# Retention chunks in another order: v scaled behind the masks, the next chunk's scores ahead, loads and copies of h in other buffers

## The chip, the core and the metric

One core of a Trainium2 chip runs the whole program. TensorE (PE) multiplies matrices from SBUF into PSUM; VectorE (DVE) and ScalarE (ACT) work element by element; GpSimd (POOL) has a small part; SyncE (SP) issues nearly all DMAs. Each engine works through its own queue in order. The metric is the device time of one execution in microseconds; smaller is better.

## What is computed

Retention (attention with a decay in place of the softmax) over 4 sequences, 8 heads, 576 positions of 64 dimensions, and behind it two layers of feed-forward, each with its own weights and function:

```python
scores = scale * np.matmul(q, k.transpose(0, 1, 3, 2))
gamma = 1.0 - 2.0 ** (-5.0 - np.arange(H))
Dmat = np.where(rel >= 0, gamma[:, None, None] ** rel[None, :, :], 0.0)
x = np.matmul(scores * Dmat, v)            # then (2304, 512): token, head and dimension
h = x @ w_in;   x = (h * np.cos(h)) @ w_out            # first layer, 512 -> 2048 -> 512
h = x @ w_in2;  x = where(h >= 1, h, where(h <= -1, 0, (h + 1) ** 2 / 4)) @ w_out2
```

All values are float32. Products are made of two parts of each operand, high and low, three matmuls for one.

## The kernel before, in words

**Tokens.** The 2304 tokens are cut into five blocks (0 and 1 have 256 and 512 tokens, the others 512) and, for retention, into 20 chunks of 128 or 64 tokens of one sequence. Chunks 0 to 6 make blocks 0 and 1, chunks 7 to 10 block 2, chunks 11 to 15 block 3, chunks 16 to 19 block 4. A *slot* is one of the 16 pieces of 128 columns of w_in for one block; the 32 slots of blocks 0 and 1 take turns and are numbered 0 to 31, of which 30 and 31 are block 1's last two.

**A chunk.** `load` fetches qk, kv and pt (a table by position). `prep` scales v by a power of gamma with the table vtb: on DVE as one instruction (line 287), in block 1 on ACT, one instruction per head (line 285). `state` multiplies k and v into a running matrix, which `add_state` adds into T (line 317; line 315 copies it for a sequence's first chunk). `scores` multiplies k and q into the banks S and O (or y0 and y1 for every second chunk of the first two blocks) and adds with `full` a part of what comes from T; `masked` multiplies by the mask msk into R (line 357); `attend` multiplies v and R and the rest of T; `post` scales by pt into xs (line 379) and splits xs into xhl, the high part on ACT (line 386) and the low part on DVE (line 387). All small matmuls of retention have line 291.

**A slot.** `mm1` multiplies xhl by wi into h, a bank of PSUM (line 413). `actA` copies h to SBUF as hs for blocks 0 and 1 (line 459) and rounds it (lines 461, 462); `actB` is a sine and a square (467, 468); `actC` multiplies by h (482) and splits the result into gh on ACT (474) and gl on POOL, for a few slots on DVE (475). `mm2` multiplies gh and gl by wo (428 to 430), two slots later. `evac` copies a finished block to st and stores it as yd.

**Weights.** They come as 64-bit words. A piece of w_in or w_out is loaded as raw (line 116, from the fifth piece on with a second copy rsh, line 122); `convert` makes C from it on DVE (149, 153), X on ACT (132), W and X on DVE (139, 140), the high part on ACT (155) and the low part on DVE (156), and the result is kept as wi or wo; wi is also stored as wd (163) for later blocks. During blocks 0 and 1 the first layer's weights are made; from block 2 on the second layer's.

**Order.** Lines 687 to 717 write out the start: loads for chunks 0 to 6 and four raw pieces, then chunk after chunk, with three conversions between. Block 2's chunks and later ones are put by a plan (`at`) at steps between slots: a load, `prep` one step before `scores`, `masked`, `attend`, `post`. A scheduler then orders the instructions of each engine by what they depend on and by its own estimate of time; a note `behind(later, earlier)` fixes an order for it, without a wait on the chip. It may move an instruction far ahead if nothing holds it. Pools set how many buffers a name has: qkv and pt (pool ap) two, x (xp) five, which hold xhl and hs, st (stp) four, raw and rsh (cv) two each.

## Time and profile before

| what | value |
|---|---|
| median of 3 runs (902.56, 901.92, 905.1) | 902.56 us |
| the profiled execution: its time, its span | 903.84 us, 902.0 us |
| busy share of the span: PE, DVE, ACT, POOL | 94%, 64%, 49%, 12% |
| DMA moved, mean | 210.87 MB, 234 GB/s |
| chain that ended last, by engine | PE 84%, DMA 7%, DVE 5%, ACT 2%, POOL 1% |
| span in 40 slices, PE busy in tenths | 5588999976989999999999999999999999999997 |
| granted clock of PE in tenths | 8588999998999999999999999999999999999999 |

The slices are 22.55 us each. A low digit of PE is time in which it waited; a low digit of the clock is time in which its matmuls ran at half speed. The chain that ended last is followed back from the last instruction to what released each step, so a stretch in which it goes over DMA, DVE or ACT is one in which PE was not what ended last.

### The profile page before, as it was taken

What the parts mean: (1) busy time and instruction counts of PE and PEld (TensorE: products, weight loads), DVE (VectorE), ACT (ScalarE), POOL (GpSimd) and SP (SyncE); (2) the same over time, 40 slices, a digit from 0 to 9 for tenths busy, and PEclk for the clock granted to TensorE, in tenths of its full rate; (3) what the DMA queues carried; (4) which work ended last, traced back from release to release, by engine and by line L of the source; (5) the groups of instructions that cost most, each with busy time, mean ns of one, the idle gap of its engine ahead of it and who ended that gap; (6) DMA issues with size and microseconds to landing.
All of it is one profiled execution on the core that took longest, in us unless ns stands there. A gap on an engine that the chain in (4) does not pass through costs nothing.

```text
span 902.0 us, 15045 instructions
## 1 busy us (share of the span) xinstructions
PE 851.3 (94%) x5740; PEld 732.6 (81%) x5740; DVE 578.1 (64%) x1107; ACT 440.8 (49%) x837; POOL 110.0 (12%) x82
## 2 busy tenths in 40 slices
PE   5588999976989999999999999999999999999997
PEld 4577888864778777788888889898898989898896
DVE  2577777635567686888688367575654577555554
ACT  3257887732545655566666544343433344433332
POOL 0025222300112221122222200000000000000000
PEclk8588999998999999999999999999999999999999
DMA  9738999744376868586987787786666766766531
GB/s 358 304 98 295 324 338 326 283 147 177 131 273 218 327 231 304 203 295 237 328 275 252 253 267 243 239 259 183 208 215 190 246 192 188 244 197 179 160 94 70
DMA packets 70694, 210.87 MB, mean 234 GB/s; under 512 B 7648, under 2 KB 12000, under 8 KB 70624
## 3 DMA queue, kind: packets, MB, share of 16 engines
q1 hardware_dynamic: 70048, 208.96, 68.3%
q8 instruction: 45, 0.74, 0.3%
q10 hardware_dynamic: 576, 0.97, 0.3%
q14 instruction: 25, 0.20, 0.1%
HBM read 169.00 MB, written 40.89 MB: 233 GB/s over the span
## 4 chain that ended last, share of the span: by engine, by line
PE 84%; DMA 7%; DVE 5%; ACT 2%; POOL 1%; issue 1%; SPq 0%; DVEq 0%; ACTq 0%
PE hq L548 19%; PE h L413 17%; PE bky L428 6%; PE bky L429 6%; PE bky L430 6%; DMA qkv<-in_kv_dram 6%; PE bky L600 5%; PE bky L601 5%; PE bky L602 5%; PE bkS L291 2%; PE bkO L602 1%; PE bkS L601 1%; PE bkO L600 1%; PE bkO L413 1%; PE bkS L413 1%; PE bkS L602 1%
## 5 line engine op out<-in xcount | busy, mean ns | idle before, releaser
L548 PE MATMUL hq<-xc,wq 128*128 128x384 f32 x1008 | 198.7, 337 | 0.5 <-DVE sC L556 0.3
L413 PE MATMUL h<-xhl,wi 128*128 128x512 f32 (+1 forms) x864 | 196.4, 374 | 0.0
L548 PEld LDWEIGHTS hq<-xc,wq 128*128 128x128 f32 x1008 | 180.0, 188 | 12.6 <-DVE sC L556 0.6
L413 PEld LDWEIGHTS h<-xhl,wi 128*128 128x128 f32 x864 | 152.6, 193 | 28.5 <-issue 0.9
L475 POOL TENSOR_TENSOR gl<-t,gh 128x512 fp32r<-128x512 f32 (+1 forms) x78 | 109.8, 1409 | 406.2 <-ACT gh L474 333.7
L474 ACT ACTIVATE gh<-t 128x384 fp32r<-128x384 f32 (+2 forms) x176 | 96.7, 550 | 92.8 <-DVE t L482 56.8
L582 ACT ACTIVATE t<-t,half 128x384 f32<-128x384 f32 x96 | 58.9, 615 | 103.2 <-DVE t L581 103.1
L428 PE MATMUL bky<-gh,wo 128*128 128x512 f32 x256 | 102.2, 399 | 3.2 <-ACT gh L474 3.2
L429 PE MATMUL bky<-gh,wo 128*128 128x512 f32 x256 | 101.0, 395 | 0.0
L430 PE MATMUL bky<-gl,wo 128*128 128x512 f32 x256 | 92.3, 391 | 0.0
L600 PE MATMUL bky<-wo,gh 128*128 128x512 f32 x192 | 75.6, 394 | 0.2 <-ACT gh L474 0.2
L601 PE MATMUL bky<-wo,gh 128*128 128x512 f32 x192 | 75.5, 393 | 0.0
L583 DVE TENSOR_TENSOR t<-t,sC 128x384 f32<-128x384 f32 x96 | 53.3, 556 | 31.2 <-ACT t L582 31.1
L467 ACT ACTIVATE t<-t 128x512 f32<-128x512 f32 (+1 forms) x80 | 46.8, 586 | 49.7 <-DVE t L462 49.1
L475 DVE TENSOR_TENSOR gl<-t,gh 128x384 fp32r<-128x384 f32 (+1 forms) x98 | 54.5, 556 | 17.9 <-ACT gh L474 17.7
L602 PE MATMUL bky<-wo,gl 128*128 128x512 f32 x192 | 61.2, 394 | 0.0
L581 DVE TENSOR_SCALAR t<-sC 128x384 f32<-128x384 f32 x96 | 34.4, 358 | 41.4 <-ACT sC L568 39.9
L428 PEld LDWEIGHTS bky<-gh,wo 128*128 128x128 f32 x256 | 49.0, 192 | 14.3 <-ACT gh L474 4.1
L429 PEld LDWEIGHTS bky<-gh,wo 128*128 128x128 f32 x256 | 49.0, 191 | 9.8
L430 PEld LDWEIGHTS bky<-gl,wo 128*128 128x128 f32 x256 | 47.7, 188 | 10.2 <-issue 0.3
L468 ACT ACTIVATE t<-t 128x512 f32<-128x512 f32 (+1 forms) x80 | 46.6, 583 | 1.5
L568 ACT ACTIVATE sC<-hq 128x384 f32<-128x384 f32 x24 | 11.7, 488 | 68.1 <-PE hq L548 68.1
(127 smaller groups left out, 1340.2 us busy)
## 6 DMA issues: line engine op xcount, KB each, us to landing
wq<-wq SPq DMA_DIRECT2D x72, 512.0 KB, 4.2
wi<-wd SPq DMA_DIRECT2D x48, 512.0 KB, 4.8
wo<-wd SPq DMA_DIRECT2D x48, 512.0 KB, 4.4
raw<-in_win_dram SPq DMA_DIRECT2D x32, 512.0 KB, 6.1
raw<-in_wout_dram SPq DMA_DIRECT2D x32, 512.0 KB, 5.7
qkv<-in_qk_dram SPq DMA_DIRECT2D x16, 512.0 KB, 6.0
wd<-wi SPq DMA_DIRECT2D x16, 512.0 KB, 5.8
wq<-tw SPq DMA_DIRECT2D x32, 256.0 KB, 4.0
```

The lines of the kernel that those rows point to most:

```text
L413: PE.matmul(hp[s][:, :n], w[:, a, kb, :], x[b][:, kb, :], start=(i == 0), stop=(i == 3 * KB - 1))
L428: PE.matmul(o, w[:, 0, es], a, start=first and e % per == 0, stop=False, skip_group_check=True)
L429: PE.matmul(o, w[:, 1, es], a, start=False, stop=False, skip_group_check=True)
L430: PE.matmul(o, w[:, 0, es], b, start=False, stop=last, skip_group_check=True)
L474: A.activation(a, u, AF.Copy)
L475: eng.tensor_tensor(out=b, in0=u, in1=f(a), op=ALU.subtract)
L548: lastmm[0] = PE.matmul(o, w[:, a, kb, :], x[b][:, kb, :], start=first and i == 0, stop=i == 5, skip_group_check=True)
L582: A.activation(t, t, AF.Square, scale=0.5, bias=half)
L583: V.tensor_tensor(out=t, in0=t, in1=h, op=ALU.max)
L600: PE.matmul(y, a[:, js], w[:, 0, :], start=n == 0, stop=False)
L601: PE.matmul(y, a[:, js], w[:, 1, :], start=False, stop=False)
L602: PE.matmul(y, b[:, js], w[:, 0, :], start=False, stop=n == NC - 1)
```

## The change

Six edits, in the order of the diff. The pool act has three buffers as its default. `load` can put its qk load behind a given instruction. `scores` takes a function that is called when its banks are named and before its first matmul; in the start this is `state`. Copies of h (hs) are made in stp and no longer in xp. In the plan, `prep` stands behind the masks of its own chunk, and a chunk's qk load stands behind the last mm1 matmul that was written by then. In the start, msk is loaded ahead of chunk 0's kv; the pt of chunks 5 and 6 has homes in act; a chunk's `prep`, `state`, `scores` and `add_state` make a stage that is written ahead of the `attend` of the chunk before; in block 0 `prep` stands behind the masks of the chunk before; the warm-up matmuls behind the masks are left out; and the first two conversions stand behind the `post` of chunks 1 and 3.

```diff
-    act = ctx.enter_context(tc.tile_pool(name="act", bufs=2))
+    act = ctx.enter_context(tc.tile_pool(name="act", bufs=LAG + 1))
...
-        def load(self, other=None, homes=None):
+        def load(self, other=None, homes=None, after=None):
...
-            SY.dma_start(out=q, in_=qk[self.i][:, :2 * NP * n])
+            i0 = SY.dma_start(out=q, in_=qk[self.i][:, :2 * NP * n])
+            if after is not None:
+                behind(i0, after)
...
-        def scores(self):
+        def scores(self, head=None):
             n = self.n
             self.Z = [bank(t) for t in self.banks]
             self.T = Ts[0]
+            if head is not None:
+                head()
             self.lastpe = None
...
-                PE.matmul(hp[s][:, :n], w[:, a, kb, :], x[b][:, kb, :], start=(i == 0), stop=(i == 3 * KB - 1))
+                lastpe[0] = PE.matmul(hp[s][:, :n], w[:, a, kb, :], x[b][:, kb, :], start=(i == 0), stop=(i == 3 * KB - 1))
...
-            hp[s] = xp.tile([P, 512], F32, tag="x", name="hs")
+            hp[s] = stp.tile([P, 512], F32, tag="st", name="hs")
...
-                    CH[i].load(homes=homes)
+                    CH[i].load(homes=homes, after=lastpe[0])
                 at(gl_, ld)
-                at(g - 1, lambda: CH[i].prep())
                 at(pos[0], lambda: CH[i].scores())
                 at(pos[0], lambda: CH[i].masked())
+                at(pos[0], lambda: behind(CH[i].prep(), CH[i].lastmask))
...
             A.dma_start(out=vtb, in_=vtab)
+            A.dma_start(out=msk, in_=mask)
             CH[i].load(A)
-            A.dma_start(out=msk, in_=mask)
...
-(wp, f"wo{k + 1}") if k < 5 else (ap, "pt")))
+(wp, f"wo{k + 1}") if k < 5 else (act, ("gh", "gl")[k - 5])))
...
+    def stage1(k):
+        c = CH[first[k]]
+        p = c.prep()
+        if c.blk == 0 and k:
+            behind(p, CH[first[k - 1]].lastmask)
+        c.scores(head=lambda: None if c.last else c.state(("y2", "y3")))
+        c.add_state()
+
+    n1 = len(first)
+    stage1(0)
+    for k in range(n1):
+        c = CH[first[k]]
         c.masked((None, "wo2")[k % 2])
-        if k < 2:
-            warm(10, c.lastpe)
-        if k + 1 < len(first):
-            prepped = CH[first[k + 1]].prep()
+        if k + 1 < n1:
+            stage1(k + 1)
         c.attend()
         if k < 2:
             warm(10, c.lastpe)
         lastpost = c.post()
-        if k == 2:
-            make_wi1(0, begin(0, 0, 0, after=prepped))
-        if k == 4:
-            make_wo1(0, begin(0, 1, 0, after=prepped))
+        if k == 1:
+            make_wi1(0, begin(0, 0, 0, after=lastpost))
+        if k == 3:
+            make_wo1(0, begin(0, 1, 0, after=lastpost))
             load_raw(0, 1, 1)
```

What the edits move on the engines is shown at three places. The line numbers of the changed kernel are 3 to 5 higher (287 is 290, 357 is 362, 379 is 384, 387 is 392, 413 is 418). First DVE in the start, before, from chunk 7's scaling to chunk 3's masks; numbers behind names tell buffers apart (qkv_2020 is chunk 7's, qkv_2025 chunk 8's):

```order
L287 TENSOR_TENSOR qkv_2020<-qkv_2020,vtb_88 128x512
L387 TENSOR_TENSOR xhl_288<-xs_385,xhl_288 128x4x128
L357 TENSOR_TENSOR R_433<-bkO_409,msk_87 128x384
L357 TENSOR_TENSOR R_433<-bkS_408,msk_87 128x384
L287 TENSOR_TENSOR qkv_2025<-qkv_2025,vtb_88 128x512
L317 TENSOR_TENSOR T_523<-bky2_483,T_430 128x128
L317 TENSOR_TENSOR T_523<-bky3_484,T_430 128x128
L379 TENSOR_TENSOR xs_464<-bkS_408,pt_173 128x256
L379 TENSOR_TENSOR xs_464<-bkO_409,pt_173 128x256
L387 TENSOR_TENSOR xhl_468<-xs_464,xhl_467 128x4x128
L357 TENSOR_TENSOR R_526<-bky1_502,msk_87 128x384
```

The change has on DVE, from chunk 0's xs to chunk 1's split (C_556 is made of the first piece of w_out, raw_189):

```order
L384 TENSOR_TENSOR xs_318<-bkS_206,pt_160 128x256
L384 TENSOR_TENSOR xs_318<-bkO_207,pt_160 128x256
L149 TENSOR_SCALAR C_556<-raw_189 128x512
L392 TENSOR_TENSOR xhl_321<-xs_318,xhl_321 128x4x128
L153 SCALAR_TENSOR_TENSOR C_556<-raw_189,C_556 128x512
L362 TENSOR_TENSOR R_425<-bkO_336,msk_87 128x384
L362 TENSOR_TENSOR R_425<-bkS_335,msk_87 128x384
L320 TENSOR_TENSOR T_375<-bky2_337,T_289 128x128
L320 TENSOR_TENSOR T_375<-bky3_338,T_289 128x128
L384 TENSOR_TENSOR xs_408<-bky0_249,pt_165 128x256
L384 TENSOR_TENSOR xs_408<-bky1_250,pt_165 128x256
L392 TENSOR_TENSOR xhl_321<-xs_408,xhl_321 128x4x128
```

The scaling of chunks 7 and 8 has left the start, chunk 2's masks now stand ahead of chunk 1's xs, and the first instruction on the piece of w_out has come ahead of them. Second, ACT in the passage from block 1 to block 2, before; the split is chunk 7's, and the copies hs behind it belong to block 1's last two slots:

```order
L434 ACTIVATE st<-bkS 128x512
L386 ACTIVATE xhl<-xs 128x4x128
L459 ACTIVATE hs<-h 128x512
L461 ACTIVATE t<-hs 128x512
L467 ACTIVATE t<-t 128x512
L468 ACTIVATE t<-t 128x512
L474 ACTIVATE gh<-t 128x512
```

And in the change, from the same copy to st on:

```order
L439 ACTIVATE st<-bkS 128x512
L472 ACTIVATE t<-t 128x512
L473 ACTIVATE t<-t 128x512
L464 ACTIVATE hs<-h 128x512
L479 ACTIVATE gh<-t 128x512
L466 ACTIVATE t<-hs 128x512
L472 ACTIVATE t<-t 128x512
L473 ACTIVATE t<-t 128x512
L479 ACTIVATE gh<-t 128x512
L464 ACTIVATE hs<-h 128x512
```

Chunk 7's split has moved from ahead of these slots to behind all of them. Third, PE where block 1 starts: before, mm1 of the first two slots lies around chunk 6's attend, and the first mm2 follows 24 matmuls of mm1 (rows from the last of them):

```order
L413 MATMUL h<-xhl,wi 128x256 x2
L428 MATMUL bkS<-gh,wo_603 128x256
L429 MATMUL bkS<-gh,wo_603 128x256
L428 MATMUL bkO<-gh,wo_603 128x256
L429 MATMUL bkO<-gh,wo_603 128x256
L413 MATMUL h<-xhl,wi 128x512 x4
L430 MATMUL bkS<-gl,wo_603 128x256
```

And in the change, behind chunk 6's attend, ahead of which eight matmuls of mm1 stand:

```order
L418 MATMUL h<-xhl,wi 128x256 x16
L418 MATMUL h<-xhl,wi 128x512 x12
L418 MATMUL h<-xhl,wi 128x256 x12
L418 MATMUL h<-xhl,wi 128x512 x12
L433 MATMUL bkS<-gh,wo_555 128x256
L434 MATMUL bkS<-gh,wo_555 128x256
L433 MATMUL bkO<-gh,wo_555 128x256
L434 MATMUL bkO<-gh,wo_555 128x256
L435 MATMUL bkS<-gl,wo_555 128x256
```

Three more slots of mm1 stand ahead of the first mm2 than before.

## Rows read from the trace of the kernel before

**Rows 1.** Stages: stretch, length, busy PE PEld DVE ACT POOL, clock, DMA share, GB/s

```profile
5.00:35.00 30.00, 17.75 (x370) 14.84 (x373) 15.40 (x34) 12.91 (x42) 0.00 (x0) 0.69 1.03 404
...
60.00:80.00 20.00, 15.46 (x76) 13.66 (x76) 18.20 (x41) 15.19 (x31) 13.17 (x3) 0.83 0.81 282
80.00:180.00 100.00, 100.00 (x588) 88.86 (x587) 73.73 (x136) 78.17 (x164) 28.15 (x26) 1.00 0.89 313
180.00:228.00 48.00, 33.84 (x512) 26.20 (x512) 19.92 (x39) 13.13 (x24) 1.29 (x1) 0.86 0.45 154
...
265.00:275.00 10.00, 7.07 (x90) 5.92 (x89) 7.40 (x15) 5.87 (x10) 2.57 (x2) 0.83 0.64 227
```

**Rows 2.** The chain that ended last, 0 to 75 us: start, length, what

```profile
58.53 0.48 DVE xhl L387
...
63.55 8.12 POOL gl L475
```

**Rows 3.** DVE's timeline, start: start, length, operation, idle time before and its end

```profile
22.81 0.42 DVE L149 TENSOR_SCALAR C<-raw 128x512 int32<-128x512 int32 x1
...
39.85 0.69 DVE L287 TENSOR_TENSOR qkv<-qkv,vtb 128x512 f32<-128x512 f32 x1 [5.40 <-DMA qkv<-in_kv_dram]
```

**Rows 4.** The chain that ended last, 180 to 275 us

```profile
180.24 2.75 PE h L413 x12
...
189.72 6.07 DMA qkv<-in_kv_dram
...
214.30 0.38 SPq L116
...
215.28 6.04 DMA raw<-in_wout_dram
...
224.77 2.00 PE h L413 x4
```

**Rows 5.** ACT's timeline in the passage from block 1 to block 2

```profile
190.46 0.63 ACT L386 ACTIVATE xhl<-xs 128x512 fp32r<-128x512 f32 x1 [10.31 <-DVE xs L379]
```

**Rows 6.** DVE's timeline in block 2

```profile
265.17 0.43 DVE L287 TENSOR_TENSOR qkv<-qkv,vtb 128x256 f32<-128x256 f32 x1 [5.61 <-DMA qkv<-in_kv_dram]
```

**Rows 7.** Groups by line and shape: count, busy us, mean ns of one, idle before

```profile
L156 DVE SCALAR_TENSOR_TENSOR wi<-C,X 128x512 fp32r<-128x512 int32 x16 | 11.6, 725 | 1.1 <-PE h L413 0.4
L387 DVE TENSOR_TENSOR xhl<-xs,xhl 128x512 fp32r<-128x512 f32 x16 | 11.6, 724 | 12.1 <-ACT xhl L386 11.9
L386 ACT ACTIVATE xhl<-xs 128x512 fp32r<-128x512 f32 x16 | 10.1, 629 | 41.7 <-DVE xs L379 41.7
...
L287 DVE TENSOR_TENSOR qkv<-qkv,vtb 128x512 f32<-128x512 f32 x13 | 9.0, 691 | 24.2 <-DMA qkv<-in_kv_dram 24.1
...
L379 DVE TENSOR_TENSOR xs<-bkS,pt 128x256 f32<-128x256 f32 x13 | 5.4, 416 | 0.0
...
L357 DVE TENSOR_TENSOR R<-bky,msk 128x384 f32<-128x384 f32 x6 | 3.0, 550 | 0.0
...
L317 DVE TENSOR_TENSOR T<-bky,T 128x128 f32<-128x128 f32 x8 | 1.9, 283 | 0.0
```

**Rows 8.** ACT's timeline, start: scaling of v of chunks 2 and 5

```profile
15.51 2.02 ACT L285 ACTIVATE qkv<-qkv,vtb 128x64 f32<-128x64 f32 x8 [5.44 <-DMA qkv<-in_kv_dram]
...
25.07 2.02 ACT L285 ACTIVATE qkv<-qkv,vtb 128x64 f32<-128x64 f32 x8 [2.35 <-DMA qkv<-in_kv_dram]
```

**Rows 9.** Waits of SP's queue, 0 to 100 us: total, times, longest

```profile
SPq L278 <- DVE R L357: 19.9, 1, 19.9
```

**Rows 10.** DVE's timeline: masks of chunks 9 and 10

```profile
209.78 0.56 DVE L357 TENSOR_TENSOR R<-bkO,msk 128x384 f32<-128x384 f32 x1 [0.87 <-PE bkS L291]
...
214.08 0.55 DVE L357 TENSOR_TENSOR R<-bkO,msk 128x384 f32<-128x384 f32 x1
```

**Rows 11.** Line 287, 180 to 400 us: idle time of DVE before it, times

```profile
  DMA qkv<-in_kv_dram: 21.2, 7
```

**Rows 12.** DVE's timeline in block 3: a scaling, and the next masks

```profile
349.31 0.69 DVE L287 TENSOR_TENSOR qkv<-qkv,vtb 128x512 f32<-128x512 f32 x1 [3.97 <-DMA qkv<-in_kv_dram]
...
357.06 0.55 DVE L357 TENSOR_TENSOR R<-bkO,msk 128x384 f32<-128x384 f32 x1
```

More of the change, by code (lines that the diff above doesn't have):

```diff
@@ L240, in retention_moe_kernel @@
     Ts = [None]
+    lastpe = [None]
     def new_x(l, n):
@@ L286, in prep @@
                 return i0
-            V.tensor_tensor(out=v, in0=v, in1=vtb[:, self.i, :u].unsqueeze(2).to_broadcast([P, u, D]), op=ALU.mult)
+            return V.tensor_tensor(out=v, in0=v, in1=vtb[:, self.i, :u].unsqueeze(2).to_broadcast([P, u, D]), op=ALU.mult)
         def mm(self, out, lhsT, rhs, start):
@@ L356, in masked @@
                 z, r = [t.rearrange("p (c m) -> p c m", c=2) for t in (self.Z[1 - j][:, :2 * w], R[:, j, :2 * w])]
-                V.tensor_tensor(out=r, in0=z, in1=msk[:, :w].unsqueeze(1).to_broadcast([P, 2, w]), op=ALU.mult)
+                self.lastmask = V.tensor_tensor(out=r, in0=z, in1=msk[:, :w].unsqueeze(1).to_broadcast([P, 2, w]), op=ALU.mult)
             self.R = R
@@ L680, in first_load @@
             A.dma_start(out=vtb, in_=vtab)
+            A.dma_start(out=msk, in_=mask)
             CH[i].load(A)
-            A.dma_start(out=msk, in_=mask)
         else:
-            CH[i].load(homes=None if k == 1 else ((wp, f"wo{19 - 2 * k}"), (wp, f"wo{18 - 2 * k}"), (wp, f"wo{k + 1}") if k < 5 else (ap, "pt")))
+            CH[i].load(homes=None if k == 1 else ((wp, f"wo{19 - 2 * k}"), (wp, f"wo{18 - 2 * k}"), (wp, f"wo{k + 1}") if k < 5 else (act, ("gh", "gl")[k - 5])))
     first_load(0)
@@ L695, in retention_moe_kernel @@
     load_raw(0, 0, 1)
-    CH[first[0]].prep()
-    for k, i in enumerate(first):
-        c = CH[i]
-        if not c.last:
-            c.state(("y2", "y3"))
-        c.scores()
+    def stage1(k):
[4 more added lines that the diff above has]
+        c.scores(head=lambda: None if c.last else c.state(("y2", "y3")))
         c.add_state()
+    n1 = len(first)
+    stage1(0)
+    for k in range(n1):
+        c = CH[first[k]]
         c.masked((None, "wo2")[k % 2])
-        if k < 2:
-            warm(10, c.lastpe)
-        if k + 1 < len(first):
-            prepped = CH[first[k + 1]].prep()
+        if k + 1 < n1:
+            stage1(k + 1)
         c.attend()
```

## Prediction

> **What bounds the kernel now.** I read the table by stages first [rows 1]. From 80 to 180 us TensorE (PE) is busy all the time at a granted clock of 1.00 (100.00 of 100): nothing is to be won there except by less PE work, and the change removes none. PE stands idle at the start (12.25 of 30 us in 5 to 35, 4.54 in 60 to 80), in the passage from block 1 to block 2 (14.16 of 48 in 180 to 228, clock 0.86), and once more in 265 to 275 (2.93 of 10). These three places are retention, a serial chain per chunk: scores (PE), masks (DVE), attend (PE), scaling by position (xs, DVE), split (xhl, ACT and DVE). So second I read the chain that ended last [rows 2, 4] and there what DVE and ACT waited for [rows 3, 5, 6].
>
> At the start DVE stands 5.40 us before L287 at 39.85 [rows 3]. That is the scaling of v of chunk 8, a chunk of block 2 that nobody needs before 180; its load was hoisted into the start and lands last. Behind it on DVE stand T and xs of chunk 2 and with them all later chunks; the last split of block 1 ends at 59.0 [rows 2]. Only then does DVE turn to the weights, without a gap, and PE waits for gl on GpSimd until 71.67 [rows 2]. In the passage L287 (chunk 11, a block ahead) again holds DVE, waiting for a load issued at 189.72 that takes 6.07 [rows 4], and ACT waits 10.31 us on chunk 7's split with the copy of h for slot 30 queued behind it [rows 5]. In 259.6 to 265.17 it is chunk 14's L287, 5.61 us [rows 6].
>
> **Part 1: the start.** Durations, a pair of two each [rows 7]: masks 1.0, xs 0.75, T 0.5; split 0.63 on ACT and 0.6 to 0.7 on DVE; scaling 0.69 on DVE, 0.25 per head on ACT (2.02 for 8 [rows 8]); of a conversion C, W and X some 0.4 each [rows 3], the product 0.7. Arrival: chunk 2's kv lands at 15.51 [rows 8] and the queues move 404 GB/s [rows 1]; the changed queue stands in the same order up to wout's first piece, which follows 2.75 MB later: 15.5 + 6.8 = 22.3 (DVE read it at 22.81 [rows 3]).
>
> The changed DVE order, walked by hand; PE's part of a chunk lies beside DVE's work in this walk except where I name it. Masks of chunks 0 and 1 end by 13.8 and xs of chunk 0 by 14.6, paced by the first loads; the exact value doesn't matter, because then DVE waits for that wout piece (C, 22.3 to 22.8): a stall of 7.7 us that the new order has put before chunk 2's masks. Split of chunk 0 and the second part of C take until 24.0. Masks of chunk 2 at 24.0, T and xs of chunk 1 by 26.2. The split of chunk 1 waits for ACT, which scales chunks 5 and 6 from 25.07 on [rows 8] (12 heads, 3.0 us): ACT splits at 28.0, DVE ends 29.4. Conversion of wi 0 and the next C, 2.5 us: masks of chunk 3 at 31.9. T, xs and split of chunk 2 end at 35.5; masks of chunk 4, then xs and split of chunk 3 at 38.2; the conversions of wo 0 and wi 1 at 40.8. Masks of chunk 5 start at 40.8; chunk 4's xs and split and a T follow; masks of chunk 6 start at 43.7; xs of chunk 5 ends at 45.0, its split at 46.3. Chunk 6's attend sits behind eight mm1 matmuls on PE: xs 47.1, and the last split ends at 48.1. Before: 59.0. The move is 10.9 us. Everything after it (C and conversions of the next weights, their loads, mm1 of block 1) hangs on that split and moves with it. I take off 0.9 for the first mm2, where PE may wait for gl (rival A): **10.0**, between 5 (the stall at gl grows by 6) and 12.5 (it vanishes with the half-clock matmuls behind it).
>
> Nothing is booked for SP, though its queue is freed: it stood at a pt load 19.9 us long [rows 9], but behind it were weight loads whose four buffers were full until the conversions after 59. Also nothing for taking chunk 7's and 8's qk out of the start: what must arrive is there in time either way. They now go late in the weight stream (1.57 MB, 3.9 us of the queues at 404 GB/s), where the DMA share is 0.89 [rows 1]; PE has no gap there and DVE, which makes the weights, 26 us idle of 100, so that is covered. If the cover were gone it would cost those 3.9 us. By the Trainium skill, "DMA: Bandwidth & Descriptors", Specifications, HBM gives one core some 358 GB/s; the 404 of this trace is above it, and the measurement decides. By the page wout's piece would land 0.9 us later and the gain would be an estimated 9 instead of 10.
>
> **Part 2: the passage.** Zero is 180.2, when block 0's last mm2 has ended and mm1 of slot 30 runs. Before, mm1 of block 2 begins at 224.77 [rows 4], 44.5 later. In the changed order no scaling and no split stands ahead of slots 30 and 31 on DVE and ACT. A 512-column matmul is 0.229 (2.75 for 12 [rows 4]); a step of small matmuls I set at 1.0 to 1.2, since masks of chunk 9 and of chunk 10 are 4.3 apart [rows 10], of which DVE has 1.75. PE: rest of mm1, mm2 and chunk 7's scores until 8.3. DVE: gl of slot 30 at 7.3, masks of chunk 7 until 8.3, scaling 9.0. mm2 until 10.8, attend until 12.6. gl of slot 31 at 13.8, xs of chunk 7 at 15.2, last mm2 at 16.5, scores of chunk 8 at 17.6, masks (behind the copies st) 19.0, scaling 19.6, attend, xs 22.9, scores of chunk 9 24, masks 25.5, scaling 26.2, attend, xs 28.2, scores of chunk 10 29.3. There the raw loads of block 2's background weights may go; before, they were issued from 214.30 on, the third landed 7.0 later (215.28 + 6.04), and DVE's C waited for it with chunk 10's xs behind [rows 4]. That knot is in the changed order too, so I carry it: 29.3 + 7.0 + 1.1 for C, xs 38.2, split 39.5, mm1 at 40.2. Gain **4.3**. Bounds: 8 if the raw loads go out earlier than C needs them; 0 if the scaling, now between masks and attend (0.69 for each of four chunks), and half clock in the gaps eat it.
>
> **Part 3: blocks 2 to 4.** The stretch 265 to 275 loses 2.93 idle and some 1.2 at clock 0.83 [rows 1], after chunk 14's L287. Scaling now stands behind that chunk's own masks, so h of the running slot passes. I take **2.5** of 4.1. The other side: 13 chunks get 0.69 between masks and attend. Where PE has mm1 and mm2 of two slots to run, as in 80 to 180, that costs nothing; uncovered everywhere it would be 9, and I carry 1 of it as the lower bound.
>
> Copies of h in stp instead of xp, four buffers instead of two: no wait on them is in the chain, so zero, as are msk ahead of kv on ACT's queue and the pt homes in act.
>
> **Sum.** 10.0 + 4.3 + 2.5 = 16.8. The profiled execution is 903.84 (span 902.0), so 887.0 against it; the median 902.56 is 1.3 lower: **885.8**.
>
> **Rivals.** A, *gl eats the start*. GpSimd's gl took 8.12 us at 63.55 [rows 2] while DVE ran without a gap. It came out when DVE stopped, because the t of slot 4 had to wait for the buffer that this gl was reading. In the changed order even the first gl falls into the gapless conversions; PE has 60 mm1 matmuls ahead of the first mm2, then only gh. I expect DVE to stop at slot 3's t (some 60 us) and PE to lose little, for 60 matmuls are 10 us of work in hand. If every gl of the first three slots is held as that one was, the start gives 5 and the time is 890.8.
>
> E, *gl is not held*. If a gl waits for one DVE instruction at most (0.7 [rows 7]) and not for eight us, PE doesn't stop after block 1's start at all, the clock stays up, and the start gives 12: 902.56 - 12 - 6.8 = 883.8. Against it stands the 8.12. So speaks the Trainium skill, "SBUF — State Buffer", Who interferes with whom: a DVE instruction with two SBUF inputs and a GpSimd one that reads SBUF shut each other out for one instruction, whoever issues first. The trace agrees that they shut each other out, not that it is for one.
>
> B, *the weight stream is the bound*. DMA share is 0.89 in 80 to 180 [rows 1]. If loads, not PE, set the pace there, the start's gain is lost: 902.56 - 6.8 = 895.8. Against: PE 100.00 of 100 at full clock.
>
> C, *no change*: the change doesn't do what it says. Of the loads that it means to hold back only qk is held: chunk 7's kv and the pt of chunks 7 and 8 (1.05 MB, 2.6 us at 404 GB/s) stay early in SP's queue, ahead of wi's third piece, and the stall on wout's piece stands before chunk 2's masks. If that carries through the chain, the start gives 1, the passage 0 and Part 3 its lower bound: 902.6.
>
> D, *slower*. A chunk's qk load may now not be scheduled ahead of a given mm1. If it slips so that kv lands after the masks, attend waits in PE's queue with mm1 and mm2 behind it, where before only DVE waited. DVE's seven such waits from 180 to 400, 21.2 us [rows 11], would be paid by PE: 902.56 + 21.2 - 16.8 = 907.0. It decides from about 8 us of slip, which is what lies between scaling and masks where they are near (349.31 to 357.06 [rows 12]).
>
> **How the numbers follow.** A difference below 0.5% (4.5 us) can't be told from none in this kernel. Forecast 0.54, A 0.17, E 0.05, B 0.09, C 0.09, D 0.06. Faster by over 0.5% holds the forecast, A, E and B: 0.85; same 0.09; slower 0.06. The range goes from 878 (12.5 + 8 + 4 off) to 897 (A's 5 and no gain in the passage, or B).
>
> **What would show it.** Right: no L287 with a wait before 60 us, last split of block 1 near 48, mm1 of block 2 some 14 us earlier than 224.77, no idle DVE stretch before L290 ahead of masks. Wrong: the last split after 53, a PE wait for gl over 5 us, gaps of PE between 70 and 165, or PE waits for L290 in blocks 2 to 4.

## Result and the profile after

| | before | after |
|---|---|---|
| median | 902.24 us (four runs, 899.97 to 905.1) | 881.5 us (four runs, 879.9 to 882.52) |
| profiled execution, its span | 903.84, 902.0 us | 882.52, 880.7 us |

The ratio is 0.9767 with a 95% interval of 0.9735 to 0.9799; predicted were 885.8 us and a range of 878 to 897. To see where the 21.3 us of the two spans lie, three marks are read from the timelines of each profiled execution; they serve for the experiments too. A is the end of block 1's last split on DVE, B the end of block 0's last mm2, C the start of mm1 of block 2.

| profiled execution | A | B | C | B to C | C to end | span |
|---|---|---|---|---|---|---|
| before | 59.0 | 180.2 | 224.7 | 44.5 | 677.3 | 902.0 |
| after | 47.8 | 167.5 | 206.1 | 38.6 | 674.6 | 880.7 |
| difference | 11.2 | 12.7 | 18.6 | 5.9 | 2.7 | 21.3 |

So 12.7 us come from the start, 5.9 from the passage from block 1 to block 2 and 2.7 from what follows. Line numbers of the changed kernel are 3 to 5 higher (287 is 290, 386 is 391, 387 is 392, 413 is 418, 459 is 464, 475 is 480).

The stages of after, with the columns of [rows 1]: stretch, length, busy time of PE, PEld, DVE, ACT and POOL, granted clock, DMA share and GB/s.

```profile
5.00:35.00 30.00, 17.45 (x458) 16.17 (x462) 14.63 (x34) 11.51 (x39) 0.00 (x0) 0.83 0.98 377
60.00:80.00 20.00, 18.98 (x113) 16.56 (x112) 18.21 (x36) 17.53 (x38) 9.03 (x6) 1.00 0.86 313
80.00:180.00 100.00, 100.00 (x602) 87.65 (x601) 70.91 (x130) 76.48 (x157) 24.20 (x23) 1.00 0.87 316
180.00:228.00 48.00, 37.07 (x594) 29.17 (x593) 25.85 (x52) 14.98 (x27) 3.87 (x3) 0.86 0.47 161
265.00:275.00 10.00, 10.00 (x81) 7.77 (x79) 8.40 (x18) 5.93 (x11) 1.86 (x2) 1.00 0.72 246
```

In 60 to 80 us PE has 3.5 us more work than in [rows 1] and the full clock (0.83 before); in 265 to 275 PE is not idle any more; 80 to 180 is full, as before. DVE's timeline in the start (start, length, operation, idle time before it and what ended it):

```profile
22.61 0.43 DVE L149 TENSOR_SCALAR C<-raw 128x512 int32<-128x512 int32 x1 [6.86 <-DMA raw<-in_wout_dram]
...
24.16 0.55 DVE L362 TENSOR_TENSOR R<-bkO,msk 128x384 f32<-128x384 f32 x1
...
28.68 0.69 DVE L392 TENSOR_TENSOR xhl<-xs,xhl 128x512 fp32r<-128x512 f32 x1 [2.45 <-ACT xhl L391]
...
40.85 1.01 DVE L362 TENSOR_TENSOR R<-bky,msk 128x384 f32<-128x384 f32 x2
...
47.41 0.43 DVE L392 TENSOR_TENSOR xhl<-xs,xhl 128x256 fp32r<-128x256 f32 x1 [0.49 <-ACT xhl L391]
```

Chunk 2's masks are there at 24.16, chunk 5's at 40.85, and the last split ends at 47.8. The 5.40 us wait of [rows 3] is gone; in the whole run DVE's scaling waits for a load once, for 1.1 us (before, ten times, 32.4 us in all). The view of who waited for whom, for line 290:

```profile
its engine sat idle before it (us, times) until:
  DMA qkv<-in_kv_dram: 1.1, 1
who waited for it (us, times):
  PEld bkS L294: 6.1, 3
  PE bkS L294: 5.5, 3
...
  PE bky L294: 2.3, 1
```

The other side of the move stands in the line of bkS: in the passage PE now waits 5.5 us, three times, with the scaling as the last thing that it waits for, between masks and attend. The masks fill part of these waits: in the chain ahead of the attend at 188.81 they have 1.00 us and the scaling 0.61. (The last line is the start, at 10.30.) The chain that ended last shows the passage (start, length, what):

```profile
167.55 1.84 PE h L418 x8
...
197.51 5.22 DMA raw<-in_wout_dram
202.76 0.44 DVE C L149
...
206.19 2.00 PE h L418 x4
...
208.59 3.71 PE h L418 x8
```

The third raw load and the conversion C behind it are still in the chain, as in [rows 4], ahead of chunk 10's xs.

### The profile page after: what moved, and what is told of

It is laid out like the page before. It is cut to its first block, busy times and chain, and to the rows that moved or that the text cites. A ratio compares the mean times of both kernels' runs of the same rounds, so it can differ in the third digit from the quotient of the medians.

```text
span 880.7 us, 15006 instructions
## 1 busy us (share of the span) xinstructions
PE 842.2 (96%) x5720; PEld 726.4 (82%) x5720; DVE 579.1 (66%) x1107; ACT 441.7 (50%) x837; POOL 104.2 (12%) x82
## 4 chain that ended last, share of the span: by engine, by line
PE 89%; DMA 4%; DVE 3%; ACT 2%; POOL 1%; issue 1%; SPq 0%; ACTq 0%; POOLq 0%
PE hq L553 19%; PE h L418 19%; PE bky L435 7%; PE bky L433 7%; PE bky L434 7%; PE bky L605 5%; PE bky L606 5%; PE bky L607 5%; PE bkS L294 2%; DMA qkv<-in_kv_dram 2%; PE bkO L294 2%; PE bkO L605 1%; PE bkO L418 1%; PE bkS L418 1%; PE bkO L607 1%; PE bkO L606 1%
## 5 line engine op out<-in xcount | busy, mean ns | idle before, releaser
L480 POOL TENSOR_TENSOR gl<-t,gh 128x512 fp32r<-128x512 f32 (+1 forms) x78 | 104.0, 1335 | 388.8 <-ACT gh L479 368.1
L479 ACT ACTIVATE gh<-t 128x384 fp32r<-128x384 f32 (+2 forms) x176 | 96.9, 551 | 84.8 <-DVE t L487 48.4
L433 PE MATMUL bky<-gh,wo 128*128 128x512 f32 x256 | 100.3, 392 | 0.0
L434 PE MATMUL bky<-gh,wo 128*128 128x512 f32 x256 | 99.9, 390 | 0.0
L435 PE MATMUL bky<-gl,wo 128*128 128x512 f32 x256 | 94.3, 392 | 1.0 <-POOL gl L480 1.0
L472 ACT ACTIVATE t<-t 128x512 f32<-128x512 f32 (+1 forms) x80 | 46.9, 588 | 43.5 <-DVE t L467 43.0
L480 DVE TENSOR_TENSOR gl<-t,gh 128x384 fp32r<-128x384 f32 (+1 forms) x98 | 54.5, 556 | 18.6 <-ACT gh L479 18.4
L433 PEld LDWEIGHTS bky<-gh,wo 128*128 128x128 f32 x256 | 48.1, 188 | 10.2 <-issue 0.3
L434 PEld LDWEIGHTS bky<-gh,wo 128*128 128x128 f32 x256 | 48.1, 188 | 9.8
```

What stands on the lines that cost most here:

```text
L433: PE.matmul(o, w[:, 0, es], a, start=first and e % per == 0, stop=False, skip_group_check=True)
L434: PE.matmul(o, w[:, 1, es], a, start=False, stop=False, skip_group_check=True)
L435: PE.matmul(o, w[:, 0, es], b, start=False, stop=last, skip_group_check=True)
L479: A.activation(a, u, AF.Copy)
L480: eng.tensor_tensor(out=b, in0=u, in1=f(a), op=ALU.subtract)
```

## Experiments

The marks of all runs, in the order of the text:

| kernel | A | B | C | B to C | C to end | span | median | ratio to before, 95% |
|---|---|---|---|---|---|---|---|---|
| scaling early | 52.6 | 172.3 | 214.1 | 41.8 | 676.2 | 890.3 | 892.99 | 0.9910 (0.9884 to 0.9936) |
| old start | 53.7 | 172.8 | 212.7 | 39.9 | 671.5 | 884.2 | 886.34 | 0.9832 (0.9810 to 0.9855) |
| three small parts undone | 48.1 | 168.0 | 211.5 | 43.5 | 673.0 | 884.5 | 887.12 | 0.9842 (0.9820 to 0.9864) |
| hs back | 48.2 | 168.0 | 211.5 | 43.5 | 672.7 | 884.2 | 886.96 | 0.9842 (0.9805 to 0.9878) |
| before, hs alone | 58.6 | 177.5 | 219.9 | 42.4 | 677.9 | 897.8 | 897.59 | 0.9967 (0.9949 to 0.9984) |
| before, scaling alone | 52.8 | 173.8 | 215.0 | 41.2 | 673.3 | 888.3 | 889.32 | 0.9872 (0.9842 to 0.9903) |
| first C behind chunk 10 | 48.1 | 167.7 | 204.7 | 37.0 | 673.5 | 878.2 | 879.99 | 0.9763 (0.9742 to 0.9785) |
| scaling ahead of masks | 48.4 | 168.1 | 206.0 | 37.9 | 672.4 | 878.4 | 880.15 | 0.9771 (0.9743 to 0.9800) |
| wout's C later | 49.1 | 173.6 | 212.5 | 38.9 | 674.1 | 886.6 | 886.94 | 0.9849 (0.9819 to 0.9880) |
| gl on DVE | 48.4 | 164.1 | 203.5 | 39.4 | 672.0 | 875.5 | 876.92 | 0.9738 (0.9701 to 0.9774) |
| wout's C later, gl on DVE | 49.0 | 166.1 | 205.9 | 39.8 | 673.3 | 879.2 | 880.32 | 0.9761 (0.9724 to 0.9798) |
| three moves together | 48.2 | 163.9 | 201.8 | 37.9 | 670.5 | 872.3 | 874.64 | 0.9714 (0.9687 to 0.9740) |

The runs before on the same chips had medians of 900.54 to 901.14 us. The marks are of one execution each; what is said of a place is read from them, what is said of the time from the medians.

### The scaling one place earlier again

```diff
+                at(g - 1, lambda: CH[i].prep())
                 at(pos[0], lambda: CH[i].scores())
                 at(pos[0], lambda: CH[i].masked())
-                at(pos[0], lambda: behind(CH[i].prep(), CH[i].lastmask))
```

> The changed kernel with one part undone: in blocks 2 to 4 the scaling of v stands again one place ahead of a chunk's scores, not behind its masks. Theory (parts 2 and 3 of the prediction): the start keeps nearly all of its gain, as only chunk 7's scaling (0.69 us) goes back into it: last split of block 1 at 47.8 to 49 us. From the end of block 0's last mm2 to mm1 of block 2 it takes again 43 to 45 us (the changed kernel 38.7, before 44.6) with DVE waits for kv loads before the scaling, and blocks 2 to 4 lose 2.8 us. Time 881.5 + 0.7 + 5 + 2.8 = 890 us (887 to 892). Rival: the old place was not what held the passage, and scaling between masks and attend costs PE the 5.5 us that it waits for the scaling from 180 to 206 us in the changed kernel: then 877 to 881 us.

892.99 us: slower than the theory's 887 to 892, and far from the rival. The waits for kv are back, ten of them with 26.1 us in all. The passage lost 3.2 us, where 5 were expected, and the rest 1.6 instead of 2.8, but the start lost 4.8, where 0.7 was expected. Only chunk 7's scaling was hoisted into it, and DVE's timeline shows why that is enough:

```profile
31.65 0.69 DVE L290 TENSOR_TENSOR qkv<-qkv,vtb 128x512 f32<-128x512 f32 x1 [6.44 <-DMA qkv<-in_kv_dram]
```

DVE comes to chunk 7's scaling before its kv has landed, and all later chunks of the start queue behind it. In the kernel before DVE came to it at 32.22 and didn't wait; there it was chunk 8's that did [rows 3]. So one scaling in the start is enough, if DVE reaches it ahead of its load.

### The old start, without the scalings in it

```diff
-    def stage1(k):
...
-    stage1(0)
...
+    CH[first[0]].prep()
+    for k, i in enumerate(first):
...
+        c.masked((None, "wo2")[k % 2])
...
+        if k + 1 < len(first):
+            prepped = CH[first[k + 1]].prep()
+        c.attend()
...
+        if k == 2:
+            make_wi1(0, begin(0, 0, 0, after=prepped))
```

> The changed kernel with the start written in the old order (masks, next chunk's scaling, attend, split, then the next chunk's scores), but still without the scalings of chunks 7 and 8 in it, and with all other parts of the change. Before, last split of block 1 ends at 59.0 us, in the changed kernel at 47.8. Theory: the start's gain has two causes of about equal size; without the 5.40 us wait and two scalings of 0.69 us about 6 of the 11.2 us stay: last split at 52 to 54 us, time 886.5 us (885 to 888.5). Rival 1, the wait for chunk 8's kv was the whole cause: split at 48 to 49, time 881 to 883 us. Rival 2, the order alone is the cause: split at 57 to 59, time 890 to 893 us.

As the theory had it: A at 53.7, 886.34 us. Of the 11.2 us at A, 5.9 are the new order, with its places for the first two conversions and without the warm-up matmuls behind the masks, which this run has again; the other 5.3 are put down to the scalings that are no longer there, a share that a later run checks. Neither rival holds.

### Three small parts undone, then one of them

```diff
-            hp[s] = stp.tile([P, 512], F32, tag="st", name="hs")
+            hp[s] = xp.tile([P, 512], F32, tag="x", name="hs")
...
-                    CH[i].load(homes=homes, after=lastpe[0])
+                    CH[i].load(homes=homes)
...
-(act, ("gh", "gl")[k - 5])
+(ap, "pt")
```

> The changed kernel with three small parts undone: the copies of h in the two-buffer pool of before, qk loads of blocks 2 to 4 not held behind the mm1 that was last, and the pt of chunks 5 and 6 in the two shared buffers, so that SP's queue stands again some 20 us at a pt load. Theory (each was booked at nothing): 880.5 to 882.5 us, last split of block 1 within 0.5 us of 47.8, TensorE full from 80 to 165 us. Rival: the freed SP queue or the held loads carry a part of the gain: 884 us or more, with the second or third pair of weights arriving later and gaps of PE between 55 and 80 us.

887.12 us: the theory that all three are worth nothing falls. The start is untouched (A 48.1, PE full from 80 to 165 but for 0.6 us), so the rival's reason falls too: the loss lies in the passage, 43.5 us instead of 38.6. So the first of the three edits was undone by itself.

> The changed kernel with one part undone: the copies of h are again in the pool of the split activations. It takes the three small parts apart, which together cost 6 us in the run with all three undone (887.1 us, passage from block 0's last mm2 to mm1 of block 2 43.7 us instead of 38.8). Theory now: the copy of slot 30 stands behind the split of chunk 7 on ACT because both come from one pool, and this alone is the loss: passage 43 to 44 us, time 885.5 to 887.5 us. Rival: the loss comes from the loads (qk early, SP blocked by a pt load): passage 38 to 40 us, time 880 to 882 us.

886.96 us and the same marks to 0.3 us: the copies of h are the whole loss, and the two other edits are worth nothing here. SP's stall did not come back with them, though: in the run with all three undone its longest wait at a pt load is 3.5 us up to 100 us, not the 19.9 of [rows 9], so what such a stall costs is not tested. ACT's timeline in the passage of this run shows the place:

```profile
178.86 0.63 ACT L391 ACTIVATE xhl<-xs 128x512 fp32r<-128x512 f32 x1 [10.91 <-DVE xs L384]
179.39 0.58 ACT L464 ACTIVATE hs<-h 128x512 f32<-128x512 f32 x1
```

It is the row of [rows 5] again, 10.31 us there, and the copy of slot 30's h is what stands behind it. In the changed kernel the same split waits 2.46 us and no copy of block 1 is behind it:

```profile
183.37 0.63 ACT L391 ACTIVATE xhl<-xs 128x512 fp32r<-128x512 f32 x1 [2.46 <-DVE xs L384]
```

ACT's order with hs in the pool x again, from the copy st of block 0 on, to be set beside the changed kernel's, in which the copies stand ahead of the split:

```
L439 ACTIVATE st<-bkS 128x512
L391 ACTIVATE xhl<-xs 128x4x128
L464 ACTIVATE hs<-h 128x512
L466 ACTIVATE t<-hs 128x512
```

The pool x holds both the copies and the pair of split activations of a block; block 2's pair is taken in the program ahead of slot 30's copy. That the shared pool is why the scheduler puts the copy behind is argued from this, not shown.

### One part of the change alone, on the kernel before

First only the copies of h in st:

```diff
-            hp[s] = xp.tile([P, 512], F32, tag="x", name="hs")
+            hp[s] = stp.tile([P, 512], F32, tag="st", name="hs")
```

> The kernel before with one part of the change alone: the copies of h in the four-buffer pool of the copies st. Theory: this moves the copy of slot 30 ahead of chunk 7's split on ACT, where before ACT stood 10.31 us; the passage from block 0's last mm2 to mm1 of block 2 falls from 44.6 to 40 to 42 us, though the scalings are still where they were, and the start stays (last split 58.5 to 59.5): 896.5 to 899 us. Rival: the wait for chunk 11's kv holds DVE as before and the passage stays at 44 us or more: 900 to 902 us.

897.59 us, inside the theory's range, but not quite by its sum: the passage takes 42.4 us, just above its 40 to 42, with 2.1 us won there, and 2.7 are won by B, which was not expected. Of these, 1.0 is PE's wait for gl, 3.54 us in this run and 4.54 before. Then only the scaling behind the masks:

```diff
-                at(g - 1, lambda: CH[i].prep())
                 at(pos[0], lambda: CH[i].scores())
                 at(pos[0], lambda: CH[i].masked())
+                at(pos[0], lambda: behind(CH[i].prep(), CH[i].lastmask))
```

> The kernel before with one part of the change alone: the scaling of v in blocks 2 to 4 behind each chunk's masks, so that chunks 7 and 8 are not scaled in the start either. Theory: the start gains 5.3 us (the part that the run with the old order kept), blocks 2 to 4 some 1.5, the passage 0 to 1, because the copy of slot 30 is still behind chunk 7's split: 893 to 895 us. Rival: the scaling was what held the passage and the start, and the other parts only tidy up: 886 to 890 us.

889.32 us: the theory was 4 us short, and the time lies in the rival's range. The rival's reason holds only in part: more than the scaling held start and passage, for the other edits are worth another 7.6 us of span (888.3 to 880.7). The start gave 6.2 at A (5.3 expected), but the passage gave 3.3, though the copy still stood behind the split (ACT waits 10.90 us there), and the rest gave 4.0. In spans the scaling alone is worth 13.7 us on the kernel before and 9.6 when taken out of the changed one; the copies 4.2 and 3.5; the order of the start 3.5. The profiled executions of before and of hs alone are among the slower ones of their kernels, so the medians are the better measure of the time: 11.2 and 11.5 us for the scaling, 3.0 and 5.5 for the copies, 4.8 for the order. The parts don't add exactly; that one hides what another leaves waiting is argued from the marks, not shown.

### The first conversion of block 2 behind chunk 10's split

```diff
-        done.append(convert(begun, t))
+        done.append(convert(begun, t, after=lastsplit.get(2)))
...
-                at(pos[2], lambda: CH[i].post())
+                at(pos[2], lambda: lastsplit.__setitem__(CH[i].blk, CH[i].post()))
```

> The changed kernel with one move on DVE: the first conversion of block 2's background weights (two instructions, for which DVE waits 3.37 us on a raw load) stands behind xs and split of chunk 10 instead of ahead of them. Theory: this is the knot that the prediction carried over; mm1 of block 2 begins at 203 us instead of 206.2 and the time falls by 3.2 us: 878.3 us (877.5 to 879.5). Rival: PE has the half clock or another wait (masks of chunk 11 at 212.9) next and the gain is given back: 881 to 882 us.

On DVE five instructions change places; the order on all other engines is the same. C, the mark, comes 1.4 us earlier and not 3.2; the time, 879.99, lies between the two theories, and its ratio can't be told from the changed kernel's. DVE's timeline shows what is late next:

```profile
202.38 0.42 DVE L384 TENSOR_TENSOR xs<-bkS,pt 128x256 f32<-128x256 f32 x1 [2.81 <-ACT T L318]
```

DVE still stands 2.81 us before xs. The releaser is an inference of the profile; what precedes xs is chunk 10's attend, whose small matmuls, from 199.63 on, take 0.47 us each, where those of chunk 7's attend, at 180.57 in the changed kernel, took 0.32. The granted clock is 0.50 in the first stretch (199.6 to 202.3) and 1.00 in the second (180.5 to 182.2); it is 0.50 around chunk 10's attend in the changed kernel, too. So about half of the knot was hidden behind an attend at half clock.

### The scaling ahead of the masks

```diff
                 at(pos[0], lambda: CH[i].scores())
+                at(pos[0], lambda: behind(CH[i].prep(), CH[i].lastpe))
                 at(pos[0], lambda: CH[i].masked())
-                at(pos[0], lambda: behind(CH[i].prep(), CH[i].lastmask))
```

> The changed kernel with the scaling of v in blocks 2 to 4 ahead of the same chunk's masks, beside its scores on TensorE, not behind the masks (and not a place ahead of the scores, as before). Theory: in the passage the scaling stands between masks and attend, PE waits 5.5 us for it there in 3 waits; some 0.5 us of each of four chunks is won: passage 36.5 to 37.5 us instead of 38.8, time 879 to 880.5 us. Rival: kv lands late and holds DVE as before, with h of the running slot behind it: 883 us or more, with DVE waits before the scaling.

The waits for kv did not grow (1.1 us in all, as in the changed kernel) and in the passage PE no longer waits for the scaling, but it waits 4.4 us for the masks instead of 5.5 for the scaling; the passage is 0.7 us shorter, not 1.3 to 2.3. The time, 880.15 us, lies in the theory's range, but the ratio, 0.9771, is that of the changed kernel. The price of the scaling's place behind the masks is thus below what a measurement can tell.

### The stall on the first piece of w_out, and gl

```diff
-            make_wo1(0, begin(0, 1, 0, after=lastpost))
+            make_wo1(0, begin(0, 1, 0, after=lastpost), after=lastpost)
```

> The changed kernel with one move on DVE in the start: both first instructions of the conversion of wout's first piece stand behind chunk 3's split, so that DVE doesn't stand 6.86 us at 15.7 us with chunk 2's masks queued behind. Theory: the chain of chunks then is limited by arrival and by ACT's scaling of chunks 3 to 6 (done at 28.0): last split of block 1 at 42 to 45 us instead of 47.8, time 876.5 to 879.5 us. Rival: DVE gets the same work later and is full from 30 to 48 us anyway, or the scaling on ACT holds the chunks: last split at 47 to 48, time 881 to 882 us.

886.94 us, 5 slower, outside both. Two things came out. The stall of 6.86 us was no price: with C gone from there, DVE waits for ACT instead, which scales chunks 3 and 4 as their kv lands. Chunk 2's masks start at 23.19 us instead of 24.16, but chunk 1's split waits for ACT again and starts at 28.79, where it was 28.68. DVE's timeline, then ACT's:

```profile
22.58 0.69 DVE L392 TENSOR_TENSOR xhl<-xs,xhl 128x512 fp32r<-128x512 f32 x1 [6.76 <-ACT xhl L391]
```

```profile
18.93 3.10 ACT L288 ACTIVATE qkv<-qkv,vtb 128x64 f32<-128x64 f32 x12 [2.63 <-DMA qkv<-in_kv_dram]
21.93 0.61 ACT L391 ACTIVATE xhl<-xs 128x512 fp32r<-128x512 f32 x1
```

And the loss is gl. GpSimd's timeline in this run, then PE's, and DVE's beside them:

```profile
53.13 7.37 POOL L480 TENSOR_TENSOR gl<-t,gh 128x256 fp32r<-128x256 f32 x2 [52.69 <-ACT gh L479]
```

```profile
59.87 0.58 PE L435 MATMUL bkS<-gl,wo 128*128 128x256 f32 x1 [6.02 <-POOL gl L480]
```

```profile
53.19 0.68 DVE L156 SCALAR_TENSOR_TENSOR wi<-C,X 128x512 fp32r<-128x512 int32 x1
...
58.55 0.68 DVE L156 SCALAR_TENSOR_TENSOR wi<-C,X 128x512 fp32r<-128x512 int32 x1
64.07 0.43 DVE L467 SCALAR_TENSOR_TENSOR t<-t,hs 128x256 f32<-128x256 f32 x1 [4.84 <-ACT t L466]
```

DVE runs thirteen instructions without a gap until 59.23, and the first two gl end 1.3 us after it stops. Taken apart, it is the first that is held; the second takes 0.72 us:

```profile
53.13 6.68 POOL L480 TENSOR_TENSOR gl<-t,gh 128x256 fp32r<-128x256 f32 x1 [52.69 <-ACT gh L479]
59.78 0.72 POOL L480 TENSOR_TENSOR gl<-t,gh 128x256 fp32r<-128x256 f32 x1
```

That is what rival A describes, and its cost here, 5.4 us by the medians, is near the 5 that A gave. In the changed kernel the same two gl took 3.60 us; there DVE stopped at 57.43 and the first of them ended at 58.01:

```profile
55.10 3.60 POOL L480 TENSOR_TENSOR gl<-t,gh 128x256 fp32r<-128x256 f32 x2 [54.66 <-ACT gh L479]
...
79.36 0.81 POOL L480 TENSOR_TENSOR gl<-t,gh 128x256 fp32r<-128x256 f32 x1 [1.80 <-issue]
```

The second row is one such gl that meets less of DVE: 0.81 us. By the Trainium skill, "SBUF — State Buffer", Who interferes with whom, whoever issues first keeps the shared ports for one instruction and the other blocks fully; the trace agrees that they shut each other out, but here GpSimd got none of twelve changes of instruction. (Which of the thirteen DVE instructions take the shared ports isn't separated by these runs.) The other way round it is one instruction: in the changed kernel a scaling that starts 0.04 us behind a gl takes 1.79 us instead of 0.68, and ends 0.5 us after that gl:

```profile
245.90 1.79 DVE L290 TENSOR_TENSOR qkv<-qkv,vtb 128x512 f32<-128x512 f32 x1
```

```profile
245.86 1.29 POOL L480 TENSOR_TENSOR gl<-t,gh 128x512 fp32r<-128x512 f32 x1 [4.42 <-ACT gh L479]
```

So gl of the first four slots was put on DVE.

```diff
-        gh[s], gl[s] = parts(u, V if pos_of[1, NC - 1] - 1 <= s <= pos_of[1, NC - 1] else G)
+        gh[s], gl[s] = parts(u, V if s < 4 or pos_of[1, NC - 1] - 1 <= s <= pos_of[1, NC - 1] else G)
```

> The changed kernel with gl of the first four slots computed on DVE instead of GpSimd, at 0.42 to 0.69 us each instead of 3.60 us for the first two and 4.50 for the next two. Theory (GpSimd's gl is held while DVE runs without a gap, as in the kernel before at 63.55): the PE waits for gl of 1.57 and 1.02 us go, DVE has 2.2 us more to do in a full stretch; end of block 0's last mm2 1 to 2.5 us earlier than 167.5, time 879 to 880.5 us. Rival: DVE is what block 1's start waits for, and 2.2 us more of it come out at the end: 881.5 to 883.5 us.

876.92 us, more than the theory gave. The interval of the ratio, 0.9701 to 0.9774, still overlaps that of the changed kernel (0.9735 to 0.9799), so the gain rests on the trace as much as on the time. DVE does such a gl in 0.41 us:

```profile
57.19 0.41 DVE L480 TENSOR_TENSOR gl<-t,gh 128x256 fp32r<-128x256 f32 x1
```

PE doesn't wait for gl at all from 48 to 165 us, and B comes 3.4 us earlier, where the two waits had been 2.6. The passage gives back 0.8, and 2.6 us of the span are won behind C, 1.0 of them in eight mm1 matmuls at block 2's start, which take 2.79 us here and 3.78 in the changed kernel. Then both moves together:

> The changed kernel with two moves: the conversion of wout's first piece behind chunk 3's split (alone it cost 5 us, with gl of the first two slots 7.37 us long on GpSimd and TensorE waiting 6.0 us for it) and gl of the first four slots on DVE. Theory: the cost was this gl and nothing else, so with gl on DVE the time is that of gl on DVE alone, 876.9, to within 1.5 us: last split of block 1 at 48 to 49 us, no wait of TensorE for gl from 48 to 80 us. Rival: the move itself delays block 1 (last split 1.2 us later, weights later): 879 to 883 us.

880.32 us, in the rival's range. Against the move alone B comes 7.5 us earlier (173.6 to 166.1), so gl was most of the cost; against gl on DVE alone it is 2.0 later. Of these 0.6 are there at A, and PE waits 1.1 us for the gl of a later slot, which is still on GpSimd and takes 5.51 us there; the remaining 0.3 are not traced.

### The three moves that helped, together

> The changed kernel with three moves together: gl of the first four slots on DVE, the first background conversion behind chunk 10's split, and the scaling of v ahead of its chunk's masks. Theory: they act at different places, block 1's start (4.6 us alone), chunk 10 (1.5) and the four chunks of the passage (1.3): 874.5 to 876 us. Rival: the two of the passage hide one another, since there TensorE's half clock is the limit: 876 to 878 us.

874.64 us, as the theory had it, and the fastest of all: ratio 0.9714 (0.9687 to 0.9740) to the kernel before, where the changed kernel's is 0.9767 (0.9735 to 0.9799). The intervals overlap by 0.0005; the five runs (874.01 to 876.27) lie below the four of the changed kernel, on a chip where the kernel before had 900.54. Against gl on DVE alone (0.9701 to 0.9774) nothing can be told from the time. The stages of this run:

```profile
60.00:80.00 20.00, 20.00 (x117) 17.68 (x116) 18.88 (x38) 17.15 (x38) 7.31 (x3) 1.00 0.96 347
180.00:228.00 48.00, 40.88 (x612) 32.78 (x611) 30.39 (x59) 18.01 (x32) 5.54 (x4) 0.86 0.53 184
```

PE is full from 60 to 80, and from 180 to 228 it has 3.8 us more work than the changed kernel; since C comes 4.3 us earlier, this is the same gain seen once more.

## Why the prediction was right, and where it was not

**Bound.** Right: the gain lies in the three named places, and 80 to 180 us stayed full at the full clock. The sum was 16.8 us; the medians are 20.7 apart, and each of the three parts came out larger than forecast.

**Part 1, 10.0 forecast, 12.7 measured.** The walk on DVE held: masks of chunk 2 predicted at 24.0 and measured at 24.16, of chunk 5 at 40.8 and 40.85, last split 48.1 and 47.8. At one place it held by luck: the stall that it put at wout's piece (22.3, measured 22.61) has a twin in ACT, which would have held DVE until 22.58 without it. The mis-sized term is the one behind the split: 0.9 was taken off for gl, but the measured move grew by 1.5 from A to B, since PE's wait of 4.5 us for gl became two of 2.6 us together, and the clock of 0.83 in 60 to 80 became 1.00. PE's waits, before and then after:

```profile
71.72 0.58 PE L430 MATMUL bkS<-gl,wo 128*128 128x256 f32 x1 [4.54 <-POOL gl L475]
```

```profile
58.06 0.39 PE L435 MATMUL bkS<-gl,wo 128*128 128x256 f32 x1 [1.57 <-POOL gl L480]
...
67.77 1.21 PE L435 MATMUL bky<-gl,wo 128*128 128x512 f32 x4 [1.02 <-POOL gl L480]
```

With that the start came out just over the upper bound of 12.5. On the cause the text named only chunk 8's scaling; the old-start run and the scaling alone on the kernel before show that the scalings are about half of the 11.2 (5.3 and 6.2), the order the other half.

**Nothing for SP and for qk.** Right as far as tested: with both undone as well as hs the run is that of hs alone (884.5 and 884.2 us of span). But SP's stall of 19.9 us did not return in that run, so for SP the zero is not shown.

**Part 2, 4.3 forecast, 5.9 measured.** The chain was right: the text has chunk 10's scores at 29.3 us after zero, the third raw load landed at 36.3 and mm1 at 40.2; measured from B they are 29.0, 35.2 and 38.6. The step that failed is the reason. The text saw slot 30's copy queued behind the split [rows 5] and let its walk have no split ahead of slots 30 and 31; but it didn't ask which edit puts the copy first, and booked "copies of h in stp instead of xp, four buffers instead of two" at zero because no wait on them was in the chain. (The pool x has five buffers, which the copies shared with the split activations; the number was not the point.) Taking them back costs 4.9 us of the 5.9 (1.9 of it come back after C, 1.2 of these in the eight matmuls that start block 2, at a higher clock): the copy stood behind the split, and the chain shows the split, not the copy. So the size came out nearly right for an edit that had been priced at nothing, which is luck as far as the sum goes. The scaling costs the passage 3.2 to 3.3 by itself; the two overlap.

**Part 3, 2.5 forecast, 2.7 measured.** Right in size, and PE's idle stretch at 265 is gone. The scaling early again gave back 1.6 of it. The sum has no term for the clock behind C, though: the eight 512-column matmuls there take 2.58 us before and 3.78 after. Without these 1.2 the part would be 3.9 (an estimate from the two rows), near the 4.1 from which the forecast had taken off.

**Rivals.** A was real but not in force: in the changed kernel DVE stopped early enough (57.4, forecast some 60), and the wout run shows what A costs where DVE does not stop, 6.0 us in one wait and 5 in the time. E, that gl is held for one instruction, is refuted by the same run, though its 12 for the start and its 883.8 are nearer to the 12.7 and the 881.5 than the forecast's 10.0 and 885.8. B: PE stayed at 100.00 of 100 with a DMA share of 0.87. D: the scaling waited for kv once, 1.1 us; PE's 5.5 us of waits are for masks and scaling, not for a load. C: no, the start gave 12.7 and not 1.

**Signs.** Of the signs of being right, the last split (47.8) came as named, and mm1 of block 2 was 18.6 us earlier, not some 14; the one wait of DVE's scaling, 1.1 us, is at 8.95, in the first chunks. Of the signs of being wrong, the last split after 53, a wait for gl over 5 us and gaps of PE from 70 to 165 did not come. One came true without the meaning that the text gave it: PE waits for line 290 in block 2, 5.5 us. With the scaling ahead of the masks these waits go and the ratio stays (0.9771), so they are no part of a loss that can be measured.

## What to carry to other kernels

An instruction that needs a late load does its harm through what is queued behind it on its engine, so a step that isn't needed for long is best held behind something that is surely later than its load. A wait in the chain names the instruction that waited, not the one that paid for it: look at the next rows of that engine, and at what pool they take their buffers from, before an edit there is booked at zero. And a stall that is removed is worth only its lead over the next wait: here 6.86 us were worth 1.0 at the next masks and nothing one split later, because the next wait, for ACT, ended 0.03 us earlier (22.58 and 22.61), and one more followed it.

## What the runs showed of the hardware

Two gl of 128x256 on GpSimd lasted 7.37 us beside a DVE without gaps, where one took 0.81 us at another time; on DVE one takes 0.41. It is not only slower but tied to the moment when DVE stops: the gl that is held ends 0.6 us after it in all three kernels that were looked at (59.81 and 59.23 in the wout run, 58.01 and 57.43 in the changed kernel, 71.66 and 71.08 before). DVE, in turn, waits for one gl that it meets (1.79 us instead of 0.68 for a scaling).

PE's clock after the passage was not expected to matter. In the changed kernel eight 512-column matmuls of block 2's mm1 take 3.78 us, in the run with three moves 2.16:

```profile
208.53 3.78 PE L418 MATMUL h<-xhl,wi 128*128 128x512 f32 x8
```

```profile
204.19 2.16 PE L418 MATMUL h<-xhl,wi 128*128 128x512 f32 x8
```

Both kernels have a stretch at half clock there (0.50, that is 1.2 GHz), and what differs is where it lies. First the changed kernel, then the run with three moves, in the columns of [rows 1]:

```profile
199.00:212.60 13.60, 10.37 (x116) 7.82 (x116) 2.88 (x6) 1.27 (x4) 0.00 (x0) 0.50 0.19 68
212.70:216.00 3.30, 3.30 (x28) 2.42 (x24) 2.22 (x4) 1.07 (x3) 0.00 (x0) 1.00 0.45 159
```

```profile
190.70:204.30 13.60, 9.96 (x173) 8.32 (x173) 6.28 (x13) 1.70 (x4) 0.00 (x0) 0.50 0.47 165
204.40:208.00 3.60, 3.60 (x22) 2.60 (x23) 1.22 (x3) 0.60 (x1) 0.00 (x0) 1.00 0.18 38
```

So 6.5 us at half clock stand behind C (206.1) in the first, and 2.5 behind C (201.8) in the second. In both the clock fell in one of PE's waits in the passage (197.43 to 199.45, and 189.22 to 190.97); why it fell at a later wait in one than in the other stays open. It moves C to end by up to 2 us (half of the 4.0 us by which the two differ behind C, an estimate), and differences of that size between runs in that column are not explained by their edits.
